# Windowed attention and a feed-forward layer on one core: larger attention units, V loads on another queue, a smaller first token block

## The chip, the cores and the metric

The kernel runs on one core of a Trainium2 chip. The metric is device time in microseconds (us), lower is better. Five engines work beside each other: TensorE (PE in the profile), ScalarE (ACT), VectorE (DVE), GpSimd (POOL) and SyncE (SP); 16 DMA engines move data. "PEld" is TensorE's weight load. Most runs of one kernel agree within about 1%; a run more than 1.5% above the fastest of its kernel counts as slow, and ratios rest on fast runs alone.

## The reference, cut to what matters

```python
# q, k, v: (batch 8, heads 8, sequence 576, head size 64), float32
scores = q @ k^T / 8                     # masked where |i - j| > 32
attn   = softmax(scores)
x      = (attn @ v), heads side by side  # 4608 tokens x 512
h      = x @ w_in                        # w_in 512 x 2048
out    = (s * relu(h)**2 + b) @ w_out    # w_out 2048 x 512
```

The two products of the feed-forward layer (FFN) are almost all of the arithmetic: 1152 matmuls of 128x128 by 512 columns. Attention is a band, so each block of keys meets few queries.

## The kernel before

The program is a graph of tasks. Each task has an engine ("stream"), an assumed cost and a key. A small planner inside the kernel simulates the graph with these costs and always takes the task that can start first:

```python
    def plan(self):
        free = {s: 0.0 for s in self.STREAMS}
        dma_free = 0.0
        # ... cut ...
            best = None
            for s in self.STREAMS:
                for t in open_[s]:
                    c = (max(free[s], t.ready), t.key, t.n)
                    if best is None or c < best[0]:
                        best = (c, t)
        # ... cut ...
            if t.dma is not None:
                dma_free = max(dma_free, st + 1300.0) + t.dma[1]
                t.fin = dma_free + 700.0
            else:
                t.fin = st + t.cost
```

The result is one fixed order of instructions on each engine; waits on semaphores are then put in for all dependences. So the assumed costs never change what is computed, only the order in which each engine does its work.

The loads, their assumed costs (650 ns to issue, 290 GB/s to move), the cast to bfloat16, and the transposes:

```python
        def load(b, n, blk, stream="sp", waits=()):
            # ... cut ...
                650.0, writes=[("STG", n, blk)], key=16 * (b - 2), waits=waits,
                dma=("l" if stream == "sp" else "a", ns * 2048 / 290.0))

        for b in range(B):
            if b > 0:
                for blk in range(NBLK):
                    for n in "qkv":
                        load(b, n, blk, waits=[wout[3]] if b == 1 else ())
            if b < 2:      # cast on VectorE, transposes on TensorE
                # ... cut ...
            else:          # cast on VectorE, transposes by DMA, issued from SyncE
                # ... cut ...
            for j in range(2 * NPAIR):
                unit(b, j % NPAIR, j // NPAIR, j)
```

A unit is one head pair by 320 or 256 queries, eight units per batch: QK on TensorE into `sc`, exp on ScalarE, the band mask multiplied in on VectorE (`ex`), row sums `ss` and `av` on TensorE, reciprocal as exp(-ln(ss)) on ScalarE, and a product into `xt` on VectorE. The FFN takes tokens in blocks of 512: `s1` (matmul `w`, relu on ScalarE, square `gt` on VectorE) and `s2` (matmul `o`, scale on VectorE, store). Its first block needs all of batch 0 up to token 511.

The softmax here doesn't subtract the row's maximum and nothing guards it: scores larger than these inputs give would overflow.

## Time and profile before

| | before |
|---|---|
| median time of 4 runs | 402.27 us (400.17 to 405.16) |
| TensorE busy | 337.9 us of 400.9 (84%) |
| first FFN matmul | 39.63 us |
| TensorE busy, 99 to 260 us | 136.2 of 161 us |

The first view is the page's row of 40 equal slices (10.0 us each): busy tenths of TensorE, the clock that it was granted, in tenths, and the busy tenths of the DMA engines.

```profile
PE   0636988892996897789796969999999999999996
PEclk9999996998799799889899989999999999999999
DMA  8999999849968978967999542310000010010112
```

From the 25th slice on TensorE is full, at full clock, and DMA soon nearly idle. Before that, DMA is mostly full and TensorE has holes; several of them, not all, come with a low clock in the same slice or the next. The second view gives the same as sums: for each stretch, the busy time of TensorE, its weight loads, VectorE, ScalarE and GpSimd (with counts), then granted clock, DMA share and GB/s.

```profile
39.60:99.00 59.40, 48.63 (x342) 21.12 (x346) 31.81 (x73) 30.18 (x45) 0.00 (x0) 0.93 0.96 173
99.00:160.00 61.00, 51.74 (x396) 22.55 (x404) 34.11 (x73) 40.52 (x67) 0.00 (x0) 0.90 0.96 176
160.00:260.00 100.00, 84.48 (x607) 37.55 (x619) 53.34 (x113) 57.88 (x90) 0.00 (x0) 0.93 0.74 152
```

Who waits for whom between 60 and 240 us (total us, times, longest):

```profile
DVE natq L375 <- DMA stgq<-in_q_dram: 41.1, 14, 8.9
...
PE ss L453 <- DVE ex L441: 20.0, 6, 7.4
```

VectorE waited 41.1 us at casts of q (`natq`) whose data had not come, and TensorE 20.0 us for masks. The two belong together, as the timeline shows; first TensorE, then VectorE, around 93 us (start, duration, what, and in brackets the idle time before and its end):

```profile
92.73 0.37 PE L429 MATMUL sc<-qt,kt 64*128 64x160 bf16 x6
100.51 0.58 PE L453 MATMUL ss<-ex,ones 128*64 128x160 bf16 x6 [7.41 <-DVE ex L441]
```

```profile
96.81 0.69 DVE L375 CAST natq<-stgq 128x1024 bf16<-128x1024 f32 x1 [8.87 <-DMA stgq<-in_q_dram]
...
99.84 0.62 DVE L441 TENSOR_TENSOR ex<-ex,mask 128x896 bf16<-128x896 bf16 x1
```

The mask stood behind a cast of a later batch. The cast waited 8.87 us for its load, and TensorE stood still for 7.41. The Trainium skill, "Perfetto Trace Analysis", section "Tensor Engine Instruction (MATMUL, LD_WEIGHTS)", says that VectorE and ScalarE are strictly first in, first out. This trace agrees for VectorE: the casts of q, k and v started at 96.81, 98.03 and 99.23 us, and only then the mask, though the exp before it had ended at 91.43 us (90.43 + 1.00).

### The profile page before, as it was taken

To read this page: it belongs to the slowest core of one execution; us is meant where nothing else is said; L and a number is where in the kernel's file an instruction comes from. 1 tells how busy PE (TensorE), PEld (TensorE's weight loads), DVE (VectorE), ACT (ScalarE), POOL (GpSimd) and SP (SyncE) were. 2 spreads that over 40 slices of the span, in tenths; PEclk is the share of its full clock that TensorE was granted. 3 is DMA by queue.
4 is the path that set the end of the run, shared out by engine and by line. 5 is a ranking of instruction groups with operands and counts; after the bars stand their busy time and mean duration, and the time that the engine had idled before them with its cause. 6 is when DMAs were issued, how large, how long until landed. Compare 5 with 4: busy or idle time off the path is not lost.

```text
span 400.9 us, 6048 instructions
## 1 busy us (share of the span) xinstructions
PE 337.9 (84%) x2358; PEld 152.7 (38%) x2400; DVE 197.7 (49%) x415; ACT 219.4 (55%) x342; POOL 14.1 (4%) x40
## 2 busy tenths in 40 slices
PE   0636988892996897789796969999999999999996
PEld 0423343341442343344342424444444444444442
DVE  6634386642662663564565355554455543333321
ACT  1547662653595387457464737677777764433310
POOL 7510000000000000000000000000000000000000
PEclk9999996998799799889899989999999999999999
DMA  8999999849968978967999542310000010010112
GB/s 169 198 204 197 170 205 215 165 80 208 228 90 198 218 138 179 206 141 157 215 192 212 137 115 66 80 41 26 29 28 28 28 52 28 26 52 28 52 52 80
DMA packets 151580, 49.43 MB, mean 123 GB/s; under 512 B 142848, under 2 KB 146944, under 8 KB 151552
## 3 DMA queue, kind: packets, MB, share of 16 engines
q1 hardware_dynamic: 141536, 43.40, 54.0%
q0 software_dynamic: 4288, 4.20, 6.4%
q10 hardware_dynamic: 5728, 1.44, 2.0%
q8 instruction: 19, 0.31, 0.3%
q14 instruction: 9, 0.07, 0.1%
HBM read 36.70 MB, written 9.44 MB: 115 GB/s over the span
## 4 chain that ended last, share of the span: by engine, by line
PE 50%; SPq 15%; DMA 8%; issue 2%; DVE 1%; ACT 1%; DVEq 0%
PE o L534 22%; PE w L517 21%; SPq L300 11%; DMA stgq<-in_q_dram 5%; SPq L383 4%; DMA stgv<-in_v_dram 3%; PE ss L453 3%; PE sc L429 2%; PE av L453 1%; SPq L549 1%; DVE ex L441 1%; ACT ex L438 0%; DVE outs L546 0%; ACT lns L464 0%; DVE gt L526 0%
## 5 line engine op out<-in xcount | busy, mean ns | idle before, releaser
L517 PE MATMUL w<-xt,win 128*128 128x512 bf16 x548 | 146.0, 392 | 4.3 <-issue 1.9
L534 PE MATMUL o<-wout,gt 128*128 128x512 bf16 x563 | 147.5, 389 | 2.0 <-issue 1.1
L517 PEld LDWEIGHTS w<-xt,win 128*128 128x128 bf16 x576 | 53.4, 100 | 68.1 <-issue 7.9
L534 PEld LDWEIGHTS o<-wout,gt 128*128 128x128 bf16 x576 | 52.6, 99 | 64.5 <-issue 5.0
L438 ACT ACTIVATE ex<-sc,zero 128x896 bf16<-128x896 f32 (+1 forms) x64 | 60.7, 949 | 9.5 <-PE sc L429 8.4
L464 ACT ACTIVATE lns<-ss,zero 128x320 f32<-128x320 f32 (+1 forms) x64 | 31.9, 499 | 50.7 <-PE ss L453 50.6
L441 DVE TENSOR_TENSOR ex<-ex,mask 128x896 bf16<-128x896 bf16 (+1 forms) x64 | 37.5, 588 | 23.0 <-ACT ex L438 22.8
L453 PE MATMUL ss<-ex,ones 128*64 128x96 bf16 (+2 forms) x384 | 25.8, 247 | 25.5 <-DVE ex L441 24.5
L375 DVE CAST natq<-stgq 128x1024 bf16<-128x1024 f32 (+2 forms) x28 | 19.4, 691 | 46.0 <-DMA stgq<-in_q_dram 44.0
L470 DVE TENSOR_TENSOR xt<-av,rec 128x320 bf16<-128x320 f32 (+1 forms) x64 | 29.1, 454 | 23.0 <-ACT rec L467 13.3
L523 ACT ACTIVATE r_28<-w,zero 128x512 bf16<-128x512 f32 x36 | 24.7, 687 | 27.3 <-PE w L517 26.1
L523 ACT ACTIVATE r_29<-w,zero 128x512 bf16<-128x512 f32 x36 | 24.7, 687 | 24.9 <-PE w L517 24.8
L523 ACT ACTIVATE r_31<-w,zero 128x512 bf16<-128x512 f32 x36 | 24.7, 687 | 21.7 <-PE w L517 21.7
L546 DVE SCALAR_TENSOR_TENSOR outs<-o,sb_36,cvec 128x512 f32<-128x512 f32 x36 | 26.9, 747 | 16.6 <-PE o L534 16.5
L467 ACT ACTIVATE rec<-lns,zero 128x320 f32<-128x320 f32 (+1 forms) x64 | 34.2, 534 | 1.4
L453 PE MATMUL av<-ex,vb 128*64 128x96 bf16 (+2 forms) x384 | 25.0, 244 | 10.0 <-DVE xt L470 10.0
L523 ACT ACTIVATE r_30<-w,zero 128x512 bf16<-128x512 f32 x36 | 24.7, 686 | 15.9 <-PE w L517 14.7
L453 PEld LDWEIGHTS ss<-ex,ones 128*64 128x64 bf16 x384 | 13.7, 116 | 50.7 <-DVE ex L441 31.0
L429 PE MATMUL sc<-qt,kt 64*128 64x96 bf16 (+2 forms) x384 | 25.0, 240 | 4.1 <-ACT ex L438 3.5
L526 DVE TENSOR_TENSOR gt<-r_29 128x512 bf16<-128x512 bf16 x36 | 15.2, 423 | 22.6 <-ACT r_29 L523 22.3
L526 DVE TENSOR_TENSOR gt<-r_30 128x512 bf16<-128x512 bf16 x36 | 15.2, 423 | 19.1 <-ACT r_30 L523 19.0
L526 DVE TENSOR_TENSOR gt<-r_31 128x512 bf16<-128x512 bf16 x36 | 15.2, 422 | 18.4 <-ACT r_31 L523 18.3
(39 smaller groups left out, 122.7 us busy)
## 6 DMA issues: line engine op xcount, KB each, us to landing
out_dram<-outs SPq DMA_DIRECT2D x36, 256.0 KB, 2.2
stgq<-in_q_dram SPq DMA_DIRECT2D x32, 256.0 KB, 5.0
stgv<-in_v_dram SPq DMA_DIRECT2D x31, 256.0 KB, 5.2
stgk<-in_k_dram SPq DMA_DIRECT2D x28, 256.0 KB, 5.1
win<-in_moe_w_in_dram POOLq DMA_DIRECT2D x4, 512.0 KB, 10.7
wout<-in_moe_w_out_dram POOLq DMA_DIRECT2D x4, 512.0 KB, 18.6
stgk<-in_k_dram ACTq DMA_DIRECT2D x4, 256.0 KB, 8.3
stgq<-in_q_dram SPq DMA_DIRECT2D x8, 128.0 KB, 4.8
```

Source lines behind the costliest of these rows:

```text
L300: lambda e: e.dma_start(STG[n][0:ns, blk, :].rearrange("p (h d) -> p h d", h=H), src_of[n][b, :, blk * 128:blk * 128 + ns, :].rearrange("h ...
L429: fns.append(lambda e, w=w, q0=q0, nq=nq, hh=hh, c0=c0: e.matmul(SC[:, hh, c0:c0 + nq], lhsT=KT[slot][64 * hh:64 * hh + 64, pr, 128 * w:12 ...
L438: add("act", lambda e: e.activation(EX[e_][:, :, 0:n], SC[:, :, 0:n], AF.Exp, bias=ZERO_F[:, :], scale=0.125), 280 + 2 * n * 0.834, reads= ...
L441: add("dve", lambda e: e.tensor_tensor(EX[e_][:, :, 0:n], EX[e_][:, :, 0:n], MASK[hf][:, :, :], ALU.mult), 170 + n / 0.96, reads=[("E", e_ ...
L453: fns.append(lambda e, q0=q0, nq=nq, hh=hh, c0=c0, i=i, dst=dst, lhs=lhs: e.matmul(dst[64 * hh:64 * hh + 64, q0 - u0:q0 - u0 + nq], lhsT=l ...
L464: add("act", lambda e: e.activation(LNS[e_][:, 0:nu], SS[:, 0:nu], AF.Ln, bias=ZERO_F[:, :], scale=1.0), 280 + nu * 0.834, reads=["SS", "Z ...
L467: add("act", lambda e: e.activation(REC[e_][:, 0:nu], LNS[e_][:, 0:nu], AF.Exp, bias=ZERO_F[:, :], scale=-1.0), 280 + nu * 0.834, reads=[( ...
L470: add("dve", lambda e: e.tensor_tensor(XT[:, pr, x0:x0 + nu], AV[:, 0:nu], REC[e_][:, 0:nu], ALU.mult), 170 + nu / 0.96, reads=["AV", ("RE ...
L517: add("pe", [lambda e, kc=kc: e.matmul(W[wb][:, :], lhsT=WIN_BF[:, kc, ft * 128:(ft + 1) * 128], rhs=XT[:, kc, t0:t0 + TOK], start=(kc == ...
L523: add("act", lambda e: e.activation(R1[rb][:, :], W[wb][:, :], AF.Relu, bias=ZERO_F[:, :], scale=1.0), 690, reads=[("W", wb), "ZERO"], wri ...
L526: add("dve", lambda e: e.tensor_tensor(GT[gs][:, ft, :], R1[rb][:, :], R1[rb][:, :], ALU.mult), 430, reads=[("R1", rb)], writes=[("GT", gs ...
L534: add("pe", [lambda e, fc=fc: e.matmul(O[ob][:, :], lhsT=GT[gs][:, fc, sub * 128:sub * 128 + 128], rhs=WOUT_BF[:, fc, :], start=(fc == 0), ...
```

## The change

Its intent: fewer and more regular attention units (192 queries by 256 keys that are shifted by 32, two head pairs each; 6 units per batch of 512 columns instead of 8 of 448 or 384); the AV product ahead of the next QK on TensorE; V, now in shifted blocks, loaded from the Pool queue to relieve SyncE; a first FFN block of 384 tokens, then one of 128, to start earlier. Two things come along and are not in its title: batch 1's transposes go from TensorE to DMA, and the planner's costs of loads are raised. (The units' priorities and gates and the order of batch 0's loads change as well.) The core of the diff:

```diff
-    NM = T // TOK
+    sizes = [384, 128]
+    while sum(sizes) < T:
+        sizes.append(min(512, T - sum(sizes)))
 # ... cut: tiles, masks, ones for the two edges ...
         def load(b, n, blk, stream="sp", waits=()):
+            if n == "v":
+                k0 = 192 * (blk // 2) - WIN + 128 * (blk % 2)
+                p0, p1 = max(0, -k0), min(128, S - k0)
-                650.0, writes=[("STG", n, blk)], key=16 * (b - 2), waits=waits,
-                dma=("l" if stream == "sp" else "a", ns * 2048 / 290.0))
+                1070.0 if stream != "pool" else 1900.0, writes=[("STG", n, blk)],
+                key=16 * (b - 2), waits=waits,
+                dma=({"sp": "l", "act": "a", "pool": "w"}[stream], ns * 9.3))
 # ... cut: load_weights ...
-                       dma=("w", 1048576 / 380.0))
+                       dma=("w", 2550.0))
 # ... cut: weights two in flight, casts one block at a time ...
-            add("pe", fns, cost + 70, reads=qk_res(b, hf), writes=["SC"], key=key, after=after,
-                name=("qk", b, j))
+            add("pe", fns, 310.0, reads=qk_res, writes=["SC"], key=key + 0.5,
+                after=after + ([("av", n - 1)] if n > 1 else []), name=("qk", n))
 # ... cut ...
         for b in range(B):
             if b > 0:
                 for blk in range(NBLK):
-                    for n in "qkv":
-                        load(b, n, blk, waits=[wout[3]] if b == 1 else ())
+                    for n in "qk":
+                        load(b, n, blk, waits=[wts[5]] if b == 1 else ())
+                for blk in range(2 * NT3):
+                    load(b, "v", blk, "pool", waits=[wts[6]] if b == 1 else ())
 # ... cut ...
-            if b < 2:
+                if b == 0:
+                    transpose_pe(b, n, blk, banks, "act" if b == 0 and n == "q" else "dve")
+                else:
+                    transpose_dma(b, n, blk)
```

## The prediction

> **What bounds the kernel now.** Three stages, by the windows view. (a) 0 to 39.6 us: TensorE (PE) is busy 17.2 us; the first feed-forward (FFN) matmul waits until all eight attention units of batch 0 are done. (b) 60 to 240 us: PE is busy 146.6 of 180 us at a granted clock of 0.91. The SyncE queue issues for 165 of 175 us (60 to 235; loads 1.04 us each, transposes 1.32). PE's main wait (waits view) is SS after the mask multiply, 20.0 us: VectorE runs in order, and a cast placed too early waits there for a q load (41.1 us in all). From 93 to 100.5 us one such cast blocks the mask, so PE. (c) 240 to 396 us: PE is busy 154 of 156 us. FFN is 1152 matmuls at 0.216 us = 249 us.
>
> After each gap of (b) matmuls run at half pace (634 against 379 ns). The Trainium skill, "TensorE: Matmul & The Clock Gate", Part 1, says an idle window of about 3.4 us halves the PE clock until PE has been busy as long; the trace agrees (clock 0.66 in 60 to 70, 1.00 throughout c). So (b) loses 33 us idle plus about 17 us of clock.
>
> **What the change does.**
> 1. Units: 8 per batch become 6. In (c) a 448-column unit costs PE 1.03 us; I estimate 1.1 for 512 columns: about 7 us saved over six batches.
> 2. AV goes before the next QK, so without FFN work to fill, a unit is a serial chain: QK to exp 0.55, exp 1.11 (estimate from 1.00 at 896 columns), mask 0.7, SS and AV 0.6: 3.0 to 3.5 us, against 1.7 in (a) now. Batch 1's six units follow each other on PE in the new order: about 19 us.
> 3. V loads on the Pool queue: SyncE per batch falls from about 32 to 27 us, below PE's 34. V rows rise from 576 to 704, DMA bytes per batch about 7%. The Trainium skill, "DMA: Bandwidth & Descriptors", "Issuing engines are not separate DMA queues", says all run on the same 16 engines. But the trace shows room: 80 GB/s while SyncE issues transposes (80 to 90 us), 204 to 227 while it issues loads.
> 4. The planner's load costs are nearer the trace, so casts stand later in VectorE's order: most of the 20 us wait should go.
> 5. The first block of 384 tokens needs 11 loads, not 15: FFN starts near 28 us.
>
> **Sum.** Blocks 0 and 1 end about 68 us (estimate), batch 1's units about 86, where block 2 begins. Left then: 8 blocks x 27.7 = 221.5, 36 units x 1.1 = 40, tail 4, stalls and cold clock 10 (now about 50). 86 + 221.5 + 40 + 4 + 10 = 362 us. Range 348 to 379. Chances: faster 0.95, same 0.04, slower 0.01.
>
> **What would show it.** First FFN matmul at 24 to 32 us; PE idle 10 to 15 us between 60 and 90; block 2 starting at 80 to 92; PE busy over 95% and clock near 1 from 95 us on; SyncE no longer issuing 94% of the time; late units at 1.1 us.
>
> **What would make it wrong.** Casts of batch 2's V stand ahead of batch 1's masks on VectorE: slow descriptor writing on Pool (I assume 1.9 us per load) would delay block 2 by 5 to 15 us and starve later batches. If batch 1's loads arrive earlier, block 2 starts before 80 us and the time is near 350.

## The result, and the profile after

| | before | after |
|---|---|---|
| median time | 402.27 us | 375.15 us (373.61 to 375.49, 4 runs) |
| first FFN matmul | 39.63 us | 31.88 us |
| start of the first FFN block that needs batch 1's data | 88.78 us | 99.25 us |
| TensorE busy, 99 to 260 us | 136.2 us | 150.7 us |

The ratio of the times is 0.931 (95% interval 0.925 to 0.938). Ratios in this text are the mean time of one kernel's fast runs over that of the other's of the same rounds, so not quite the ratio of the quoted medians. The changed kernel is 6.9% faster and inside the predicted range, but 13 us later than the 362 us forecast.

The same rows of the page as before; a slice is now 9.3 us:

```profile
PE   1277985935499999988898899989999999999996
PEclk9999998975599999999999999999999999999999
DMA  8979999999999999999899798863000001001012
```

The many holes of the first 24 slices have become one large hole in the 9th to 11th and small ones before and after it. The same stretches:

```profile
39.60:99.00 59.40, 39.08 (x336) 22.69 (x338) 30.11 (x78) 26.02 (x47) 18.21 (x23) 0.80 1.18 208
99.00:160.00 61.00, 59.66 (x460) 27.76 (x468) 39.35 (x90) 42.99 (x62) 10.11 (x12) 0.97 1.19 198
160.00:260.00 100.00, 91.08 (x748) 42.82 (x758) 62.10 (x139) 67.26 (x100) 8.51 (x10) 1.00 0.93 171
```

From 39.6 to 99 TensorE does less than before (39.1 us against 48.6), and at a lower clock; after 99 it does more. The large hole is batch 1's six units, which stand alone in TensorE's order (timeline of TensorE, L435 is QK, L525 and L543 are the FFN):

```profile
70.78 4.48 PE L543 MATMUL o<-wout,gt 128*128 128x512 bf16 x20
75.20 0.40 PE L435 MATMUL sc<-qt,kt 64*128 64x128 bf16 x8
...
81.47 0.61 PE L435 MATMUL sc<-qt,kt 64*128 64x128 bf16 x8
84.11 0.64 PE L458 MATMUL ss<-ex,ones 128*64 128x128 bf16 x8 [2.03 <-DVE ex L445]
84.54 0.63 PE L458 MATMUL av<-ex,vb 128*64 128x128 bf16 x8
85.11 0.61 PE L435 MATMUL sc<-qt,kt 64*128 64x128 bf16 x8
...
99.25 6.95 PE L525 MATMUL w<-xt,win 128*128 128x512 bf16 x23 [3.27 <-DVE xt L472]
```

From QK at 81.47 to QK at 85.11 one unit takes 3.64 us, of which TensorE works about 1.6 us, at half pace (0.61 us for a QK that takes 0.40 elsewhere). Block 2 of the FFN, the first that needs batch 1, starts at 99.25 us.

What the waits view showed before has shrunk, here from 99 to 260 us, where the kernel before had 26.7 us at casts of q and 20.0 us for masks. A wait of QK for transposes of k by DMA that had not landed (3.7 us) is new:

```profile
DVE natq L379 <- DMA stgq<-in_q_dram: 10.6, 12, 2.2
...
PE sc L435 <- DMA kt<-natk: 3.7, 2, 2.0
PE ss L458 <- DVE ex L445: 3.6, 3, 1.6
```

### The profile page after: what moved, and what is told of

It is laid out like the page before. It is cut to its first block, busy times and chain, and to the rows that moved or that the text cites. A ratio compares the mean times of both kernels' runs of the same rounds, so it can differ in the third digit from the quotient of the medians.

```text
span 373.8 us, 6108 instructions
## 1 busy us (share of the span) xinstructions
PE 319.2 (85%) x2385; PEld 155.5 (42%) x2424; DVE 193.2 (52%) x439; ACT 206.4 (55%) x310; POOL 44.7 (12%) x62
## 4 chain that ended last, share of the span: by engine, by line
PE 54%; DMA 19%; SPq 9%; DVE 7%; ACTq 3%; ACT 3%; issue 2%; DVEq 0%
PE o L543 25%; PE w L525 22%; DMA stgq<-in_q_dram 12%; DMA stgk<-in_k_dram 7%; SPq L300 6%; ACTq L300 3%; SPq L387 3%; PE ss L458 3%; PE sc L435 2%; DVE ex L445 2%; PE av L458 2%; ACT ex L442 1%; DVE xt L472 1%; DVE vb L379 1%; DVE gt L534 1%
## 5 line engine op out<-in xcount | busy, mean ns | idle before, releaser
L525 PE MATMUL w<-xt,win 128*128 128x512 bf16 (+2 forms) x624 | 146.4, 367 | 5.5 <-DVE xt L472 4.2
L543 PE MATMUL o<-wout,gt 128*128 128x512 bf16 x554 | 141.5, 382 | 6.0 <-DVE cvec L567 4.0
L525 PEld LDWEIGHTS w<-xt,win 128*128 128x128 bf16 x640 | 59.4, 100 | 71.8 <-issue 5.1
L543 PEld LDWEIGHTS o<-wout,gt 128*128 128x128 bf16 x576 | 53.2, 98 | 65.5 <-DVE cvec L567 4.2
L442 ACT ACTIVATE ex<-sc,zero 128x1024 bf16<-128x1024 f32 x48 | 53.2, 1109 | 12.1 <-PE sc L435 12.1
L445 DVE TENSOR_TENSOR ex<-ex,mask 128x1024 bf16<-128x1024 bf16 x48 | 33.0, 688 | 33.2 <-ACT ex L442 32.7
L300 POOL DMA_DIRECT2D stgv<-in_v_dram x42 | 35.7, 853 | 120.5 <-DVE vb L379 111.5
L465 ACT ACTIVATE lns<-ss,zero 128x384 f32<-128x384 f32 x48 | 27.7, 578 | 27.6 <-PE ss L458 27.5
L531 ACT ACTIVATE r_29<-w,zero 128x512 bf16<-128x512 f32 (+2 forms) x40 | 25.7, 643 | 30.7 <-PE w L525 30.6
L458 PE MATMUL ss<-ex,ones 128*64 128x128 bf16 x384 | 22.1, 244 | 20.5 <-DVE ex L445 20.1
L531 ACT ACTIVATE r_28<-w,zero 128x512 bf16<-128x512 f32 (+2 forms) x40 | 25.7, 642 | 23.1 <-PE w L525 22.6
L531 ACT ACTIVATE r_31<-w,zero 128x512 bf16<-128x512 f32 (+2 forms) x40 | 25.7, 644 | 23.0 <-PE w L525 22.0
L531 ACT ACTIVATE r_30<-w,zero 128x512 bf16<-128x512 f32 (+2 forms) x40 | 25.7, 643 | 19.2 <-PE w L525 18.8
L472 DVE TENSOR_TENSOR xt<-av,rec 128x384 bf16<-128x384 f32 x48 | 26.5, 552 | 11.5 <-ACT rec L468 11.2
L458 PEld LDWEIGHTS ss<-ex,ones 128*64 128x64 bf16 x384 | 13.6, 119 | 39.6 <-DVE ex L445 26.7
L468 ACT ACTIVATE rec<-lns,zero 128x384 f32<-128x384 f32 x48 | 29.3, 610 | 0.8
L435 PE MATMUL sc<-qt,kt 64*128 64x128 bf16 x384 | 21.2, 237 | 9.0 <-ACT qt L407 5.3
L534 DVE TENSOR_TENSOR gt<-r_29 128x512 bf16<-128x512 bf16 (+2 forms) x40 | 15.8, 396 | 22.7 <-ACT r_29 L531 22.7
L534 DVE TENSOR_TENSOR gt<-r_31 128x512 bf16<-128x512 bf16 (+2 forms) x40 | 15.8, 396 | 22.3 <-ACT r_31 L531 22.0
L534 DVE TENSOR_TENSOR gt<-r_30 128x512 bf16<-128x512 bf16 (+2 forms) x40 | 15.8, 394 | 18.6 <-ACT r_30 L531 18.6
```

Source lines behind the costliest of these rows:

```text
L300: lambda e: e.dma_start(STG[n][p0:p1, blk, :].rearrange("p (h d) -> p h d", h=H), src_of[n][b, :, s0:s0 + ns, :].rearrange("h s d -> s h d ...
L435: fns.append(lambda e, u=u, pr=pr, a=a, hh=hh: e.matmul(SC[:, hh, 256 * u + 128 * a:256 * u + 128 * a + 128], lhsT=KT[slot][64 * hh:64 * h ...
L442: add("act", lambda e: e.activation(EX[e_][:, :, :], SC[:, :, :], AF.Exp, bias=ZERO_F[:, :], scale=0.125), 1130.0, reads=["SC", "ZERO"], w ...
L445: add("dve", lambda e: e.tensor_tensor(EX[e_][:, :, :], EX[e_][:, :, :], MASK[:, :, :], ALU.mult), 700.0, reads=[("E", e_), "MASK"], write ...
L458: fns.append(lambda e, u=u, a=a, hh=hh, dst=dst, lhs=lhs: e.matmul(dst[64 * hh:64 * hh + 64, 192 * u + 64 * a:192 * u + 64 * a + 128], lhs ...
L465: add("act", lambda e: e.activation(LNS[e_][:, :], SS[:, 0:384], AF.Ln, bias=ZERO_F[:, :], scale=1.0), 600.0, reads=["SS", "ZERO"], writes ...
```

## The experiments

Two rival accounts of the gain stood at the start. One: the parts named in the title bring it (V off SyncE, larger units, an early start). The other: the planner's new costs bring it, by moving casts behind masks. And for the missing 13 us: the serial unit chain, or the late arrival of batch 1's data.

One caution for all runs: every edit makes the planner order all instructions anew. A difference of a few us between two versions can be an accident of the order. All runs gave correct results. Each ratio is against runs of the kernel before on the same chip in the same rounds.

### The planner's costs alone, in the kernel before

```diff
-                650.0, writes=[("STG", n, blk)], key=16 * (b - 2), waits=waits,
-                dma=("l" if stream == "sp" else "a", ns * 2048 / 290.0))
+                1070.0, writes=[("STG", n, blk)], key=16 * (b - 2), waits=waits,
+                dma=("l" if stream == "sp" else "a", ns * 9.3))
-                       dma=("w", 1048576 / 380.0))
+                       dma=("w", 2550.0))
```

> The kernel before with nothing changed but the planner's costs of loads (1.07 us issue, 9.3 ns a row, 2.55 us a weight load): the same instructions in another order. The run with the old costs in the changed kernel lost 20 of its 27 us. Theory P (the plan is most of the gain, in either kernel): VectorE's casts move behind the masks, the 20.0 us wait of SS on the mask falls below 8, the time falls by 15 to 25 us, to 376 to 386. Rival (the plan only pays with the new units, because the old unit order leaves the same waits): within 5 us of 401.

Measured: 375.37 us, ratio 0.9375 (0.933 to 0.942). That is the whole gain of the change (0.931) from three numbers that no instruction carries out. (The three were not tested one by one.) TensorE's waits from 60 to 240 us hold only this for the masks:

```profile
PE ss L453 <- DVE ex L441: 0.3, 1, 0.3
```

20.0 us have become 0.3, and no cast waits for a load any more in that stretch. The same two late stretches:

```profile
99.00:160.00 61.00, 58.79 (x484) 26.74 (x492) 40.17 (x86) 48.05 (x80) 0.00 (x0) 1.00 0.94 178
160.00:260.00 100.00, 98.36 (x750) 44.26 (x764) 62.81 (x129) 72.50 (x114) 0.00 (x0) 1.00 0.90 176
```

TensorE is busy 157.2 of these 161 us, where it was 136.2, and the clock is full. And it had all this although its first FFN matmul came at 49.99 us, 10 us later than in the kernel before.

### The old costs, in the changed kernel

```diff
-                1070.0 if stream != "pool" else 1900.0, writes=[("STG", n, blk)],
+                650.0 if stream != "pool" else 1900.0, writes=[("STG", n, blk)],
-                dma=({"sp": "l", "act": "a", "pool": "w"}[stream], ns * 9.3))
+                dma=({"sp": "l", "act": "a", "pool": "w"}[stream], ns * 2048 / 290.0))
-                       dma=("w", 2550.0))
+                       dma=("w", 1048576 / 380.0))
```

> The changed kernel with the planner's old costs of loads (650 ns issue, 290 GB/s; one part undone; it moves instructions only). Prediction point 4: most of the old waits come from casts placed too early because loads were thought fast. If so, casts stand earlier in VectorE's order again, block the masks, and PE's wait of SS on the mask from 100 to 250 us goes from 3.6 us to 15 us or more: the time rises by 8 to 20 us. Rival: V on Pool and the smaller first block did it, and the time stays within 4 us.

Measured: 394.22 us, ratio 0.981 (0.976 to 0.986). 19 of the 27 us are lost. The wait of `ss` on the mask from 99 to 260 us is back:

```profile
PE ss L458 <- DVE ex L445: 21.3, 8, 5.7
```

The two runs agree from both sides: the new costs carry nearly all of the gain. All other parts together, the helpful and the harmful ones netted, add 0.6% with the new costs (0.9375 to 0.9314) and 2% with the old ones (0.981); that they hide a gain and losses of their own is seen further down.

### V on Pool alone, in the kernel before

```diff
-                        load(b, n, blk, waits=[wout[3]] if b == 1 else ())
+                        load(b, n, blk, "pool" if n == "v" else "sp",
+                             waits=[wout[3]] if b == 1 else ())
```

(The load's cost and queue follow the stream, as in the changed kernel; other costs stay old.)

> The kernel before with V of batches 1 to 7 issued on the Pool queue and nothing else changed (old planner's costs). Prediction point 3 (SyncE's issue time, 165 of 175 us, is a limit): the time falls by 5 to 15 us. Rival D (the DMA engines are shared and V on a second queue takes its share out of turn): same or slower, 400 to 410, and q and k loads and transposes take longer to land than 5.0 and 2.5 us.

Measured: 394.32 us, ratio 0.986 (0.980 to 0.993), a small gain. Both sides were partly right. The time fell by about 6 us, as point 3 of the prediction would have it. But q loads took 5.7 us to land (5.0 before) and transposes 3.9 (2.5 before), as the rival expected.

### V back on SyncE, in the changed kernel

```diff
-                    for n in "qk":
-                        load(b, n, blk, waits=[wts[5]] if b == 1 else ())
-                for blk in range(2 * NT3):
-                    load(b, "v", blk, "pool", waits=[wts[6]] if b == 1 else ())
+                for n, blk in order:      # q0 k0 q1 k1 v0 v1 q2 k2 k3 v2 v3 ...
+                    load(b, n, blk, waits=[wts[6 if n == "v" else 5]] if b == 1 else ())
```

> The changed kernel with V loaded on the SyncE queue for batches 1 to 7, in the same order as the casts (one part undone). My prediction held that moving V to Pool relieves a SyncE queue that is the limit; but in the changed kernel SyncE still issues for 145 of 151 us from 99 to 250, as busy as before. Theory C (SyncE is the limit, V on Pool is worth much): six more loads of about 1.05 us per batch, 34 us per batch against PE's 34; stalls return between 100 and 250 us and the time rises by 8 to 20 us. Rival D (the 16 DMA engines are the limit; SyncE is only held up by them): time within 4 us of the changed kernel, and batch 1's q and k loads, no longer behind six V loads issued at once at 45.5 us, land earlier (the 7.0 us wait of the cast at 52 us goes).

Measured: 363.87 us, ratio 0.906 (0.903 to 0.909), 11 us faster than the changed kernel. Neither number expected came: theory C had it slower, and rival D within 4 us. But the more loaded SyncE went with the faster kernel, so its issue time was not the limit here. From 99 to 250 us it issued for 143.6 of 151 us with V on Pool and for 139.6 of 151 us with V on SyncE (counting only what lies inside the stretch), though it then carried 118 loads and transposes in that time instead of 107. Its issue time stretches and shrinks: a transpose took about 1.55 us to issue with V on Pool (88.1 us for 57) and 1.40 with V on SyncE (70.2 us for 50). I had read the time of a queue that is held up as work of its own. Block 2 started at 98.01 us, so most of the gain came later: TensorE was busy 98.6 us of the 100 from 160 to 260, against 91.1, and its waits there for transposes of k are gone.

The edit also changes the order among loads, to the order of need; this run alone does not tell the queue from the order. The next one does so in part.

### V on Pool, but held back

```diff
-                        load(b, n, blk, waits=[wts[5]] if b == 1 else ())
+                        own[n, blk] = load(b, n, blk, waits=[wts[5]] if b == 1 else ())
                 for blk in range(2 * NT3):
-                    load(b, "v", blk, "pool", waits=[wts[6]] if b == 1 else ())
+                    load(b, "v", blk, "pool", waits=[own["k", (1, 3, 4)[blk // 2]]]
+                         + ([wts[6]] if b == 1 else []))
```

> The changed kernel, V still on the Pool queue, but each pair of V loads waits until the last k block of the same batch that its unit needs has landed, so that V can no longer run ahead of q and k. V on SyncE gave 364 against 375. Theory D1 (out of turn: V of a later batch, free to run ahead, takes a share of the engines from q, k and transposes that are needed first): 362 to 368, transposes land in about 2.5 us again. Rival D2 (Pool's own descriptor writing or its traffic is what costs): stays at 373 to 378. Holding V back could add a wait of its own for V, seen as a mask or AV that waits for a V cast.

Measured: median of four runs 365.57 us, but two of them (366.92 and 367.63) count as slow, over 1.5% above the fastest; the fast ones took 360.24 and 364.23 us, ratio 0.905 (0.896 to 0.914). V is still on Pool, and about 12 us are gained. A cause shows on SyncE's own queue, at batch 1's q and k loads. In the changed kernel Pool issues six V loads from 45.5 to 50.5 us, and SyncE then does:

```profile
47.67 5.80 SPq L300 DMA_DIRECT2D stgq<-in_q_dram  x1
53.51 5.20 SPq L300 DMA_DIRECT2D stgk<-in_k_dram  x1
...
61.89 0.64 SPq L300 DMA_DIRECT2D stgk<-in_k_dram  x1
```

With V held back the corresponding third pair, the last load and the first transpose are:

```profile
46.52 3.70 SPq L300 DMA_DIRECT2D stgq<-in_q_dram  x1
50.27 0.85 SPq L300 DMA_DIRECT2D stgk<-in_k_dram  x1
...
54.10 0.63 SPq L300 DMA_DIRECT2D stgk<-in_k_dram  x1
54.78 1.45 SPq L387 DMA_TRANSPOSE qt<-natq  x1
```

The last load of the batch is issued 7.8 us earlier, batch 1's first QK comes at 66.57 us instead of 75.20, and block 2 starts at 89.69 instead of 99.25. So in this plan it is V's running ahead, out of turn, that cost time. That it does so by taking the shared engines from loads that are needed first is my reading of the longer issues, not tested apart; and beside transposes on TensorE the same edit cost time (the third version below). One part of the expectation was wrong: transposes took 6.0 and 5.6 us to land, not 2.5, with V now running beside them; batch 1's first QK waited 1.33 us for one.

### QK free to go first again

```diff
-            add("pe", fns, 310.0, reads=qk_res, writes=["SC"], key=key + 0.5,
-                after=after + ([("av", n - 1)] if n > 1 else []), name=("qk", n))
+            add("pe", fns, 310.0, reads=qk_res, writes=["SC"], key=key,
+                after=after, name=("qk", n))
```

> The changed kernel, but the next QK may go before the AV again (one part undone). In the changed kernel block 2 of the FFN starts at 99.25 us, and batch 1's six units run alone from 75.2 to 96 us at 3.6 us each. Theory A (the serial unit chain is what delays block 2): two units overlap, about 2.3 us each (ScalarE's exp, ln and reciprocal), so block 2 starts near 91 us and the time falls by 6 to 9 us, to about 367. Rival B (the arrival of batch 1's data delays it, the chain only fills a wait): block 2 stays within 2 us of 99 and the time within 2 us of 375. If QK first costs elsewhere, in the late stage from 250 us, PE would show gaps there, which it does not now (118.0 busy of 119).

Measured: two fast runs of 369.03 and 370.84 us, ratio 0.922 (0.917 to 0.927), so about 1% faster than the changed kernel's 0.931 (0.925 to 0.938), with intervals that overlap. A third run, 375.22 us at a lower clock, counts as slow. The fourth, the profiled one, took 1111.93 us; there is thus no trace of a normal run, and where the 1% comes from stays open. (That odd run is told of at the end.) Less than the 6 to 9 us of theory A, more than rival B: neither is shown.

### Batch 1's transposes on TensorE

```diff
-                if b == 0:
-                    transpose_pe(b, n, blk, banks, "act" if b == 0 and n == "q" else "dve")
+                if b < 2:
+                    transpose_pe(b, n, blk, banks if b == 0 else banks[2:],
+                                 "act" if b == 0 and n == "q" else "dve")
```

> The changed kernel, but batch 1's ten q and k transposes are done on TensorE as in the kernel before, not as DMA transposes (one part undone). In the changed kernel they are issued on SyncE only after the last of batch 1's loads, 62.6 to 76.1 us, and the planner puts all six units of batch 1 behind blocks 0 and 1. Theory B (batch 1 is late because its transposes queue behind its loads): the units interleave with blocks 0 and 1, block 2 starts at 80 to 90 us and the time falls by 8 to 18 us, to 357 to 367. Theory A (only the serial chain matters): the units still take 3.6 us each but with FFN work between them; the gain would then also appear, so this run alone does not separate A from B; with the run that puts QK first it does. If loads themselves are the limit (last one lands about 66 us, block 0 and 1's work ends at 75): block 2 not before 85.

Measured: 362.28 us, ratio 0.903 (0.899 to 0.907): 13 us faster than the changed kernel. Batch 1's units now lie among the work of blocks 0 and 1. Block 2 started at 93.57 us with its predecessors' work partly beside it, and TensorE was then busy 60.1 of 61 and 98.2 of 100 us in the two late stretches. The time is as theory B has it, block 2's start is not (80 to 90 us). And about half of the gain lies where batch 1 is long done: against the changed kernel TensorE was busy 7.8 us more from 40 to 99 us, and 7.1 us more from 160 to 260, though V still ran free on Pool. So the unnamed part of the change, DMA transposes for batch 1, was a loss in this plan, but only half of the gain lies where the edit aimed; by what way the new order brought the rest was not traced.

### Blocks of 512 from the start

```diff
-    sizes = [384, 128]
+    sizes = [512]
 # and the gate of a unit, mapped to the new block numbers:
+                        r = r // 2 if r < 32 else r - 16
```

> The changed kernel with blocks of 512 tokens from the start (one part undone; the units' gates are mapped to the new block numbers). Prediction point 5 (the smaller first block lets the FFN start early): first FFN matmul goes from 31.9 to 38 to 42 us. If that start is on the critical path the time rises by 6 to 10 us. Rival: block 2's start waits for batch 1 anyway (99 us), the early start only fills time in which PE would wait, and the time stays within 3 us of the changed kernel's 375.

Measured: 370.2 us, ratio 0.926 (0.920 to 0.932). The first FFN matmul moved from 31.88 to 39.78 us and block 2 from 99.25 to only 99.83; the time did not rise but fell slightly, within the intervals. An early FFN start is worth nothing here, because what follows waits for batch 1.

### Versions that beat both kernels

The first puts V on SyncE and batch 1's transposes on TensorE, both edits as above.

> The changed kernel with V on SyncE (364 alone) and batch 1's transposes on TensorE (362 alone). If the two gains have different causes (V out of turn after 160 us; batch 1's transposes behind its loads before 100 us) they add: 350 to 356, with block 2's units mixed into blocks 0 and 1 and no PE gaps from 100 us. If both only remove the same DMA crowding around batch 1, the time stays at 360 to 364.

Measured: 356.6 us, ratio 0.886 (0.879 to 0.892). The two gains add for the most part; block 2 starts at 86.32 us. Compare it also with the kernel before with new costs alone (0.9375): both have V on SyncE, batch 1's transposes on TensorE and the new costs. What this version has beyond that (the larger units, AV before QK, the smaller first block, another order of loads and casts) is thus worth about 5% together (0.886 against 0.9375). So these parts of the change did pay; V on Pool and the DMA transposes of batch 1 had hidden it. How the 5% divides was not tested.

The second adds two earlier starts:

```diff
-            wait = [first["k", 3]] if i == 0 else [first["v", 5]] if i == 1 else [wts[i - 2]]
+            wait = [first["k", 3]] if i == 0 else [first["k", 3]] if i == 1 else [wts[i - 2]]
-                                 "act" if b == 0 and n == "q" else "dve")
+                                 "act" if b == 0 and n == "q" and blk > 1 else "dve")
```

> The run above, and two starts moved: the second weight load no longer waits for the last V of batch 0 but for its fourth k block as the first does (DMA moved only 110 to 117 GB/s between 18 and 27 us in the changed kernel), and q blocks 0 and 1 of batch 0 leave PSUM by VectorE, because ScalarE is held up issuing loads until 15 us (its wait of 12.4 us before the first copy). First QK at 11 to 12 us instead of 15.7, weights complete 4 to 6 us earlier. If the start is on the critical path: 3 to 8 us below the run above. If the time to batch 1's data is what counts and the DMA engines are full, within 2 us of it.

Measured: 353.7 us, ratio 0.877 (0.872 to 0.882), the fastest of all. But not for the reason given: the first QK moved from 15.50 to 11.58 us as expected, yet the first FFN matmul stayed at 31.74 (31.64 in the run above) and block 2 at 86.09. The 1% shows up later, as 59.6 busy us instead of 57.9 from 99 to 160; it may be only a luckier order.

The third is the first with V on Pool and held back instead of on SyncE.

> The changed kernel with V on Pool but held back until the k block that its unit needs has landed (366 alone, 360 to 368), and batch 1's transposes on TensorE (362 alone). If holding V back and V on SyncE are the same cure, this lands within 4 us of V on SyncE with the same transposes. If Pool has a value of its own (SyncE's issue time freed), it is faster than that by 3 us or more.

Measured: 371.29 us, ratio 0.921 (0.916 to 0.926), 15 us slower than V on SyncE. It is also 9 us slower than transposes on TensorE with V running free on Pool (362.28 us, 0.903). So holding back gained about 12 us in one plan and cost 9 in another. TensorE was busy 54.3 of the 61 us from 99 to 160, where the V-on-SyncE version had 57.9. The largest wait there is the old fault again, a mask behind a cast of q whose data had not come:

```profile
145.65 0.43 DVE L379 CAST natq<-stgq 128x512 bf16<-128x512 f32 x1 [4.97 <-DMA stgq<-in_q_dram]
145.99 0.68 DVE L445 TENSOR_TENSOR ex<-ex,mask 128x1024 bf16<-128x1024 bf16 x1
...
146.73 0.41 PE L458 MATMUL ss<-ex,ones 128*64 128x128 bf16 x8 [3.67 <-DVE ex L445]
```

Casts of q waited 10.1 us in that stretch, against 3.6 with V on SyncE. This stall of 3.67 us is about as long as the loss of the stretch; where the rest of the 15 us goes stays open.

The fourth is the second with QK free to go first.

> The fastest version so far (354: V on SyncE, batch 1's transposes on TensorE, two starts moved), with the next QK again free to go before the AV. Theory A says that AV first costs where units run alone, as batch 1's six did (3.6 us each). Here batch 1's units have FFN work between them; only batch 0's first four still run alone. So if A is right, at most 2 to 5 us are left to gain, from an FFN start at 26 to 29 us instead of 31.7; if block 2's start (86 us) hangs on batch 1's data, nothing: within 2 us of 354. If AV first is worth something late, as its author may have meant (VectorE and ScalarE kept in step), it is slower by 2 us or more.

Measured: 357.86 us, ratio 0.892 (0.883 to 0.902), 1 to 2% slower than the second. (Four of its seven reference runs count as slow and are left out.) The first FFN matmul came at 33.65 us, later, not earlier. So AV before QK may have cost about 1% in the changed kernel, and its removal cost 1 to 2% in this one; neither is a rule.

## Why the prediction was right or wrong

**The total.** The forecast was 86 (start of block 2) + 275.5 (the rest). Measured: 99.25 + 274.5 us to the end of the span. The second term was right almost to the microsecond (TensorE idled 14.5 us in that time; the forecast had 10 for stalls and 4 for the tail), the first was mis-sized by 13 us, and that is the whole difference to 375.

**Block 2's start.** "Blocks 0 and 1 end about 68 us (estimate), batch 1's units about 86." The first ended near 75, in part because batch 1's casts stalled VectorE in the middle of block 1's work: one waited 6.99 us for a q load that V loads had pushed back, and the scaling `cvec` behind it kept TensorE waiting 3.98 us:

```profile
59.13 0.43 DVE L379 CAST natq<-stgq 128x512 bf16<-128x512 f32 x1 [6.99 <-DMA stgq<-in_q_dram]
...
60.61 1.04 PE L543 MATMUL o<-wout,gt 128*128 128x512 bf16 x4 [3.98 <-DVE cvec L567]
```

The units took 24 us (75.20 to 99.25), not 18: 17.1 us from the first QK to the sixth, and then 6.9 us until block 2 could start, because the last unit still had its whole chain to go and its product `xt` stood behind two casts of later data (about 1.5 us). With V held back block 2 started 10 us earlier; batch 1's transposes on TensorE brought 13 us of the total.

**Point 1, units.** Right in size: from the `ss` at 276.71 to that at 283.00 us lie one unit and 24 FFN matmuls; 6.29 - 24 x 0.216 = 1.11 us per unit, forecast 1.1. Its worth in the total was not tested alone; it is one of the parts that make up the 5% above.

**Point 2, the serial chain.** Right in kind. From QK to QK the first step took 2.90 us (75.20 to 78.10), at full clock; from the third on, at half clock, a step took 3.6 us, above the forecast of 3.0 to 3.5, because the matmuls of a step took longer (`ss` 0.64 us instead of 0.41). Letting QK go first brought about 1%, within the intervals and without a trace to show where.

**Point 3, V on Pool.** This is the step that failed. "SyncE per batch falls from about 32 to 27 us, below PE's 34" took issue time for a limit. With V on Pool SyncE still issued for 143.6 of 151 us; with V put back, 139.6 of 151, and the kernel was 11 us faster. The longest issues (5.80 and 5.20 us) came while and after Pool issued six V loads; with V held back they were 3.70 and 0.85. (Pool issued those six in 5.08 us by the profile, not at the 1.9 us each that the prediction feared.) The page that the prediction cited, "DMA: Bandwidth & Descriptors" in the Trainium skill, says under "Issuing engines are not separate DMA queues" that only the sequencer's time is saved; the runs fit this: with V on Pool q loads took 5.8 us to land, with V on SyncE 4.6. They add that V on a second queue can take its turn ahead of more urgent loads. In the kernel before, with its bad plan, V on Pool still gained 1.4%; so its sign depends on the plan.

**Point 4, the planner's costs.** Right, and much too small in the text, where it was one item of five. Three constants alone made the kernel before as fast as the whole change: 375.37 us, ratio 0.9375 against 0.9314.

**Point 5, the early start.** The start came as forecast (31.88 us, range 24 to 32), but was worth nothing: with blocks of 512 the FFN starts 8 us later and the kernel is no slower, and with new costs in the old kernel it starts at 49.99 us and the time is the same.

**The clock.** That waits cost clock too was right, the picture of it too narrow. By the Trainium skill, "TensorE: Matmul & The Clock Gate", Part 1, an idle window of about 3.4 us halves TensorE's clock. The unit stage, where TensorE had gaps of only about 2 us between short matmuls, shows a granted clock of 0.50 from 80 to 100 us; after 110 us it is 1.00. The kernel before fits no rule by gap length either. Its clock fell to 0.50 near 60.7 us with no gap over 0.74 us from 52 us on, but with TensorE busy for only 0.93 of the 2 us from 58 to 60; and after a gap of 3.25 us at 215.64 us the `ss` ran at full pace (0.36 us; 0.58 after the gap of 7.41).

**The signs named in advance.** First FFN matmul: came true. Block 2 at 80 to 92: no, 99.25. TensorE idle 10 to 15 us between 60 and 90: 9.4 us, nearly. Busy over 95% from 95 us on: true to 160 (59.66 of 61), not from 160 to 260 (91 of 100). SyncE no longer issuing 94% of the time: false, 95%.

## What to carry to other kernels

Where a scheduler fixes the order of instructions, its cost model is part of the kernel: compare its assumed load times with the trace before you rebuild the computation, and look for an in-order engine that waits at work placed too early. A queue that is always issuing is not thereby the limit; see whether its issues are longer than when it runs alone. And loads that move to a queue of their own can overtake more urgent ones. One queue in order of need paid here in both plans tried; holding the loads back on a second queue paid in one and cost in the other. When such a change comes with many parts, undo each part alone before you believe in any, and then in pairs: the gains need not add.

## What the Trainium skill lacked or had wrong

- "DMA: Bandwidth & Descriptors" (section "Issuing engines are not separate DMA queues") says that the time to initiate a DMA is usually small relative to the DMA itself. In the changed kernel a SyncE load took 0.37 us to issue at 41.98 us, as the first after a pause of 26 us on that queue, and 5.80 us at 47.67 us, with other loads under way; a q load took 5.8 us from issue to landing. SyncE was issuing 95% of the time without being the limit. For local loads the page does not say that a queue's issue time can be time in which it is held up.
- The same page gives no warning that an engine's own work stands behind loads that it issues slowly: in the changed kernel ScalarE's first copy waited 12.44 us, until 14.54 us, behind seven loads that it issued itself.
- "TensorE: Matmul & The Clock Gate", section "HAM oscillation", gives as its abstract rule that TensorE should have no idle gap over about 3.4 us; the section after it knows of a clock that swings with frequent short idles, but gives no length for them. In the changed kernel the clock halved between 78.10 us (a QK of 0.40 us) and 80.43 (an `ss` of 0.64 us, L458, 0.41 at full clock) and stayed so until after 100 us, with no gap longer than 2.04 us until 96. TensorE was busy about 1.0 of the 3.2 us before the fall (75.6 to 78.8). Such short bursts between gaps of 2 us did not keep the clock up.
- The same page mentions, under "HAM trace caveats", a clock found stuck at a quarter for over 50 us and unreliable records of it. One run here (QK free to go first) took 1111.93 us: a 512-column matmul took 0.82 us from start to start (8 in the 6.56 us from 909.26 to 915.82) instead of 0.216, for nearly the whole run, with a recorded clock of 1.00. Three other runs of the same kernel took 369 to 375 us. The cause was not tested. The record is doubtful at the start of the ordinary runs too: it says 1.00 for the first 40 us of the kernel before, yet the first four FFN matmuls there took 1.91 us (39.63), where four take 1.03 later (88.78).

```profile
909.26 3.52 PE L525 MATMUL w<-xt,win 128*128 128x512 bf16 x4
912.46 3.68 PE L543 MATMUL o<-wout,gt 128*128 128x512 bf16 x4
915.82 3.52 PE L525 MATMUL w<-xt,win 128*128 128x512 bf16 x4
```
